# Attention with a mixture of experts on one core: routing rounds seven slots apart in the steady phases, digit sums over 128 rows, and weight subtractions and token low parts at other steps

## The chip, the cores and the metric

The kernel runs on one core of one Trainium2 chip. The metric is the device time of one execution in microseconds (us), the median of the timed runs. Engines: PE is TensorE, DVE is VectorE, ACT is ScalarE, POOL is GpSimd, SP is SyncE.

## The reference

```python
def reference(**inputs):                       # cut
    # attention: 4 batches, 8 heads, 768 positions, head size 64; a query sees the keys
    # whose 6 signs of k @ proj are the same as those of q @ proj
    x = attn_out.transpose(0, 2, 1, 3).reshape(3072, 512)
    logits = x @ w_gate                        # 3072 tokens, 8 experts
    order = np.argsort(-logits.flatten())
    for idx in order:                          # greedy: the best pairs first
        tok, e = idx // 8, idx % 8
        if assigned[tok] >= 0 or counts[e] >= 384: continue
        assigned[tok] = e; counts[e] += 1
    for e in range(8):
        h = np.maximum(x[assigned == e] @ w1[e], 0)    # 512 -> 1024
        out[assigned == e] = h @ w2[e]                 # 1024 -> 512
```

The assignment is greedy over all 24,576 logits, each expert takes 384 tokens, and the products are kept close to fp32 by splitting each operand into an fp16 high part and an fp16 low part.

## The kernel before

**Attention** fills the first 430 us or so. A written table puts its work at numbered steps; constants for the experts' part are made there too, one every four half steps from 89 on (`late`, L350), most of them on POOL.

**Experts.** The greedy assignment is done in eight phases. A phase finds the expert that is full next, its threshold logit, and the 384 tokens that it gets. A threshold is a key of 32 bits, found in six digits (`WID`, 7 bits and then five times 5): a *round* for a digit compares (L493, DVE, `zcmp`), counts per expert by matmul (L504 for the first digit, L511 for others), subtracts from what is left (L513, L514), marks which thresholds are passed (L589) and whether any is (L590, `zhit`), sums the marks over partitions with a one column matmul (the digit sum, L593), and adds the digit to the key (L597, DVE, `zd`). For the digits after the first the marks lie in 32 partitions, and the digit sum reads 32 rows. After the last digit L607 and L608 sum once more, L613 to L631 on DVE work out who is a member (L700 the rows of the expert's weights), L634 and L635 number the members on PE, L643 and L669 build one-hot tables on DVE, L645 collects the token indices on PE, and L661 to L667 close the phase; the next phase starts with L475 to L493.

**Stages and slots.** While phase p is routed, the tokens of the expert before go through its two layers on PE. This is a *stage* of 68 slots: slots 0 to 31 are `layer1` (three matmuls of 384 columns each, L775), slots 32 to 67 `layer2` (two matmuls of 512 columns each, L787). Phase p is spread over stage p-1 and the end of the stage before. `run` puts everything else at slots by tables: `EV[p]=(c0,R)` gives a phase's first slot and the distance R of its rounds, the count of round l at `c0+6+R*l` and its digit sum at `c0+9+R*l`; then come the last sum, L634 and L645 (phase 1 has its own table `E1`; phases 5 and later use `EV[0]`). All engines execute their own instructions in the order of the slots, so an instruction that waits holds up all behind it on its engine.

**Weights.** `wload` fetches an expert's w1 (2 MB) with an indirect DMA from POOL's queue (L716) as soon as the phase knows the expert (L700); ACT splits it in four quarters (L725 the high part, L726 the scaled copy), and the low part is `f - h`, eight subtractions of 128x512 for each weight. These wait in a list, `s.pend`. Three places take from it: `fill` (one subtraction on DVE, L741), `hand` (so many on POOL after a digit's compare, L737, by the tables `H1` and `HS`; the one element copy L736, `ztick`, makes POOL wait for that compare), and the due slot (L847, POOL: whatever is not taken by then). ACT also makes the digits' scaled copies for DVE (L579, `zE`), the tokens' high parts (L750, `xh`), the relu (L777, `hh`) and the outputs (L790); DVE makes the low parts of tokens (L751, `xl`) and of the hidden layer (L778, `hl`).

```python
def hand(s,n):
    n=min(n,len(s.pend))
    if n: s.nc.gpsimd.tensor_copy(s.z([1,1],F32,"tick"),s.gate)
    for _ in range(n): s.nc.gpsimd.tensor_tensor(*s.pend.pop(0)[1],op=ALU.subtract)
```

Of the kernel before, what the change touches and what calls it, by code (L numbers as in the profile page):

```python
# [380 lines left out]
E1=[-12,-4,-3,2,6,8,10,13,16,19,22,25,28,31,34,37,42,49]  # L381
H1=[0,0,0,0,0,1,0,2,0,2,0,2,0,2,0,0,0,0]
EV=[(-17,8),(0,0),(-5,7),(-8,7),(-12,7)]
WL=[4,46]
# [5 lines left out]
XS=[56,56,57,57]  # L390
XD=[0,8,7,4]
KW=[1,0,4,0,2,19,7,1]
SC=16
XSC=8.0
WSC=64.0
class Moe:
# [6 lines left out]
    def consts(s):  # L403
# [33 lines left out]
        todo.append(lambda: G_.tensor_scalar(s.wtb,wt,-32.0,2.0**-44,op0=ALU.add,op1=ALU.mult))  # L437
        s.tiny=fill([128,1],2.0**-32,"tiny",BF).to_broadcast([128,128])

        s.gp=cp.tile([128,2,2,NC],BF,name="gp")  # L440
# [98 lines left out]
    def phase(s,ph):  # L539
# [9 lines left out]
        if not last:  # L549
# [13 lines left out]
            for l,w in enumerate(WID):  # L563
# [3 lines left out]
                if l==0 or first:  # L567
                    for c0,c1_ in blocks if first else ((0,NC),):
                        if l: s.compare(cmp,l,d,c0,c1_)
                        s.count(pc,P,cmp,l,c0,c1_)  # L570
                    if first:
                        if l==0: wp=s.wps(); s.warm(KW[7],wp)
                        s.warm(KW[0],wp)
                    for a,b in ((l+1,l+2),) if first else ((1,6),):
                        if a<6:
                            for q in range(a,b): s.digit(P,q,slice(0,NC))
                            if first: V.tensor_tensor(E[:,a:b],D[:,a:b],s.sc[:,a:b],op=ALU.mult)
                            else:
                                for q in range(a,b): nc.scalar.activation(E[:,q],D[:,q],AF.Copy,scale=2.0**-sum(WID[:q+1]))  # L579
                                s.fill()  # L580
                else:
                    nt=s.count4(pc,P,cmp)

                if l==5: break
                sat=t([128,8],BF,"sat"); hit=t([128,1],BF,"hit"); J=NT[l]
                if l==0 or first:
# [5 lines left out]
                pn=ps(); n=pn[:,0:1]  # L592
                T.matmul(n,s.us[l][0:J],hit[0:J],start=True,stop=True)  # L593
                if first: s.warm(KW[1],wp)
                elif l==0: s.fill()
                d2=t([128,NC],BF,"d2",bufs=6); s.gate=d2[0:1,0:1]
# [4 lines left out]

            sat=t([128,8],BF,"satl"); s.gate=sat[0:1,0:1]; nn=t([128,1],F32,"nn"); nf=t([128,1],F32,"nf")
            if first: V.tensor_scalar(sat[0:32],pc[0:32,0:8],0.0,None,op0=ALU.is_ge)
# [3 lines left out]
            T.matmul(pe[:,0:8],s.ones,s.wtb,start=True,stop=False)  # L607
            T.matmul(pe[:,0:8],s.tiny[0:32],sat[0:32],start=False,stop=True)  # L608
            if first: s.warm(KW[2],wp)
# [133 lines left out]
    def xsplit(s,ph,d):  # L743
        if d==0:
            s.W[ph,'x']=(s.t([128,4,384],F16,"xh",bufs=1),s.t([128,4,384],F16,"xl",bufs=1))
        xh,xl=s.W[ph,'x']
        px=s.psX.tile([128,512],F32,name="px")
        for c in range(3):
            s.nc.tensor.transpose(px[:,c*128:c*128+128],s.XG[ph][:,c,d*128:d*128+128],s.identf)
        s.nc.scalar.mul(xh[:,d],px[:,0:384],XSC)  # L750
        s.lag.append((s.now+3,lambda: s.nc.vector.scalar_tensor_tensor(xl[:,d],px[:,0:384],XSC,xh[:,d],op0=ALU.mult,op1=ALU.subtract)))  # L751

# [63 lines left out]
    def run(s):  # L816
# [7 lines left out]
        for p in range(1,8):  # L824
# [3 lines left out]
            for l in range(4): c+=[c0+6+R*l,c0+9+R*l]  # L828
            c+=[c0+6+4*R,c0+9+4*R,c0+15+4*R,c0+23+4*R]
            ev=[b+e for e in (E1 if p==1 else c)]  # L830
            hs=H1 if p==1 else HS
            dec=ev[-3]
# [72 lines left out]
```

## Time and profile before

| | |
|---|---|
| median of 3 runs | 759.65 us (759.64 to 762.48) |
| the profiled execution's own time | 763.7 us |
| its span, first to last instruction | 761.9 us |
| mean granted TensorE clock | 0.966 of full speed |
| busy share | PE 90%, DVE 72%, POOL 65%, ACT 61%, PEld 58% |
| the expert part with its eight stages | from 444.3 us to 753.5 us |

The shares are means over stretches with different limits. The experts' part is read stage by stage: how long a stage is, what PE waits for in it, and what that engine waits for in turn.

### The profile page before, as it was taken

The numbers are of one execution on the slowest core, as the hardware profiler recorded it, in microseconds if no ns is written. First come the engines' busy times: TensorE is split into PE (matmuls) and PEld (weight loads), VectorE is DVE, ScalarE is ACT, GpSimd is POOL, SyncE is SP. The second block draws the span as 40 slices with busy tenths as digits, with TensorE's granted clock in tenths as the row PEclk, the third lists the DMA queues.
The fourth block names the chain that finished last, engine by engine and source line by source line (L and its number), as shares of the span: only waits on it lengthen the run. The fifth ranks groups of instructions, "written<-read, shape, count | busy, mean of one in ns | idle before, by whom it ended". The sixth has DMA issues, their size and how long they took to land. (4 is left out here: it accounts for less than half of the span.)

```text
span 761.9 us, 19025 instructions
## 1 busy us (share of the span) xinstructions
PE 687.1 (90%) x7789; PEld 440.1 (58%) x7789; DVE 550.4 (72%) x1180; ACT 465.7 (61%) x852; POOL 493.2 (65%) x431
## 2 busy tenths in 40 slices
PE   8898889999999999997888669988989899999995
PEld 2566666767767677675566445544545455555452
DVE  4879968889888898987765666788777878653120
ACT  6677665777776777754554063755646475756550
POOL 8596849696886968855564236374747383858661
PEclk9999999999999999999999569999999999999999
DMA  7638653526445274330001250707071617162711
GB/s 187 174 107 207 154 153 97 149 74 165 133 110 137 74 176 121 88 76 22 22 12 34 65 199 17 261 29 268 37 257 48 220 72 265 43 232 84 260 44 41
DMA packets 39951, 93.57 MB, mean 123 GB/s; under 512 B 4548, under 2 KB 30520, under 8 KB 37816
## 3 DMA queue, kind: packets, MB, share of 16 engines
q1 hardware_dynamic: 33048, 46.21, 23.2%
q0 software_dynamic: 6816, 46.15, 17.3%
q8 instruction: 61, 1.00, 0.6%
q14 instruction: 26, 0.21, 0.1%
HBM read 59.53 MB, written 12.58 MB: 95 GB/s over the span
## 5 line engine op out<-in xcount | busy, mean ns | idle before, releaser
L255 POOL TENSOR_TENSOR lo<-pt 128x768 f16<-128x768 f32 x143 | 233.5, 1646 | 81.5 <-ACT pt L252 72.1
L252 ACT ACTIVATE pt<-pst 128x384 f32<-128x384 f32 x384 | 182.8, 491 | 97.8 <-PE pst L251 85.0
L228 DVE TENSOR_REDUCE m<-pss 128x1 f16<-128x770 f32 x192 | 182.5, 956 | 43.5 <-PE pss L226 42.1
L250 PE MATMUL pst<-qa,ka 128*128 128x384 f16 x384 | 125.9, 328 | 5.5 <-DVE XT L294 3.1
L251 PE MATMUL pst<-qb,kb 128*128 128x384 f16 x384 | 125.9, 328 | 0.0
L267 PE MATMUL psv<-vh,lo 128*128 128x65 f16 x1152 | 122.0, 195 | 3.4 <-POOL lo L255 3.4
L266 PE MATMUL psv<-vl,pt 128*128 128x64 f16 x1152 | 122.2, 194 | 0.0
L265 PE MATMUL psv<-vh,pt 128*128 128x65 f16 x1152 | 122.2, 195 | 0.0
L265 PEld LDWEIGHTS <-pt 128*128 128x128 bf16 x1152 | 107.3, 98 | 12.9 <-issue 3.5
L266 PEld LDWEIGHTS <-pt 128*128 128x128 bf16 x1152 | 106.4, 99 | 9.8 <-issue 0.3
L226 PE MATMUL pss<-ka,qa 128*128 128x385 f16 x384 | 95.3, 330 | 14.9 <-DVE m L228 13.3
L267 PEld LDWEIGHTS <-lo 128*128 128x128 f16 x1152 | 106.5, 98 | 3.7 <-POOL lo L255 3.6
L725 ACT ACTIVATE wh<-wf 128x1024 f16<-128x1024 f32 x64 | 67.2, 1050 | 39.8 <-PE psa L693 21.1
L737 POOL TENSOR_TENSOR wl<-wf,wh 128x512 f16<-128x512 f32 x64 | 72.1, 1146 | 0.0
L775 PEld LDWEIGHTS <-wh 128*128 128x128 f16 x512 | 48.3, 98 | 37.2 <-issue 8.3
L726 ACT ACTIVATE wf<-wf 128x1024 f32<-128x1024 f32 x62 | 65.5, 1057 | 2.0
L778 DVE SCALAR_TENSOR_TENSOR hl<-px,hh 128x384 f16<-128x384 f32 x64 | 34.7, 552 | 42.7 <-ACT hh L777 42.3
L226 PEld LDWEIGHTS <-qa 128*128 128x128 f16 x384 | 37.5, 98 | 46.6 <-issue 24.3
L787 PEld LDWEIGHTS <-hh 128*128 128x128 f16 x384 | 36.7, 99 | 43.5 <-issue 6.3
L255 DVE TENSOR_TENSOR lo<-pt 128x768 f16<-128x768 f32 x49 | 60.8, 1241 | 1.5 <-ACT pt L252 1.0
L790 ACT ACTIVATE o<-po 128x512 f32<-128x512 f32 x24 | 14.3, 594 | 70.4 <-PE po L787 70.3
L775 PE MATMUL px<-xh,wh 128*128 128x384 f16 x256 | 55.5, 329 | 1.7 <-DVE xl L751 1.4
(250 smaller groups left out, 1334.5 us busy)
## 6 DMA issues: line engine op xcount, KB each, us to landing
vp<-in_vv_dram SPq DMA_DIRECT2D x8, 768.0 KB
x_dram<-X SPq DMA_DIRECT2D x16, 384.0 KB
qp<-in_qT_dram SPq DMA_DIRECT2D x7, 768.0 KB
kp<-in_kT_dram SPq DMA_DIRECT2D x7, 768.0 KB
qa<-qh SPq DMA_DIRECT2D x14, 192.0 KB
ka<-kh SPq DMA_DIRECT2D x14, 192.0 KB
qb<-qh SPq DMA_DIRECT2D x14, 192.0 KB
kb<-kh SPq DMA_DIRECT2D x14, 192.0 KB
```

Of the source, the lines that this page charges most:

```text
L226: T.matmul(ps[:,hf,0:HK],QA[u][:,j,qc*128:qc*128+128],KA[u][:,j,hf*HK:hf*HK+HK],start=True,stop=True)
L228: V.tensor_reduce(M6[h][:,qc:qc+1],ps[:,:,0:HK],axis=AX.XY,op=ALU.max,negate=True)
L250: T.matmul(ps[:,0:384],KA[u][:,j,kr],QA[u][:,j,r],start=True,stop=False)
L251: T.matmul(ps[:,0:384],KB[u][:,j,kr],QB[u][:,j,r],start=False,stop=True)
L252: A.activation(PT[h,kc][0][:,r],ps[:,0:384],AF.Exp,scale=0.125)
L255: eng.tensor_tensor(l,p,p.bitcast(BF)[:,1::2],op=ALU.subtract)
L265: T.matmul(av[:,c,:],ph[:,r],VH[u][:,j,kc,:],start=(kc==0 and c==0),stop=False,skip_group_check=True)
L266: T.matmul(av[:,c,0:64],ph[:,r],VL[u][:,j,kc,:],start=False,stop=False,skip_group_check=True)
L267: T.matmul(av[:,c,:],l[:,r],VH[u][:,j,kc,:],start=False,stop=False,skip_group_check=True)
L725: s.nc.scalar.mul(h[:,r],f[:,r],WSC)
L737: for _ in range(n): s.nc.gpsimd.tensor_tensor(*s.pend.pop(0)[1],op=ALU.subtract)
L775: T.matmul(p[:,0:384],a[:,o:o+128],b[:,d],start=n==0,stop=n==11)
```

## The change

- Phases 5 and 6 (`EV[0]`): rounds 7 slots apart, not 8. The last sum is then at slot 20 of the stage (24 before), L634 at 26 (30), L645 at 35 (38), for phase 7 too. In phases 2 to 4 L645 comes one slot later.
- Digit sums after the first digit, and the last sum, read 128 rows: `hit` and `satl` are kept tiles whose other rows are zero, made by three more memsets on POOL among the constants.
- Weight subtractions: phase 1 hands 2, 2, 2, 3, 3 to POOL (1, 2, 2, 2, 2 before) and takes none on DVE in its first digit; phases 2 and 3 hand 3, 3, 3, 4 (2, 3, 3, 3 before). Phases 4 and later keep `HS`.
- Tokens: phase 1's transposes come two slots later; the low parts `xl` follow the transposes after one slot (phase 1) or two, not three.

```diff
-H1=[0,0,0,0,0,1,0,2,0,2,0,2,0,2,0,0,0,0]
-EV=[(-17,8),(0,0),(-5,7),(-8,7),(-12,7)]
+H1=[0,0,0,0,0,2,0,2,0,2,0,3,0,3,0,0,0,0]
+H2=[0,0,0,3,0,3,0,3,0,4,0,0,0,0]
+EV=[(-17,7),(0,0),(-5,7),(-8,7),(-12,7)]
-XD=[0,8,7,4]
+XD=[0,10,7,4]
+        s.hits=[fill([128,1],0.0,f"hit{i}",BF) for i in range(2)]; s.satl=fill([128,8],0.0,"satl",BF)
-                                s.fill()
+                                if ph>1: s.fill()
-                sat=t([128,8],BF,"sat"); hit=t([128,1],BF,"hit"); J=NT[l]
+                sat=t([128,8],BF,"sat"); hit=t([128,1],BF,"hit") if l==0 or first else s.hits[l%2]; J=NT[l]
-                T.matmul(n,s.us[l][0:J],hit[0:J],start=True,stop=True)
+                T.matmul(n,s.us[l][0:J if first else 128],hit[0:J if first else 128],start=True,stop=True)
-                elif l==0: s.fill()
+                elif l==0 and ph>1: s.fill()
-            sat=t([128,8],BF,"satl"); s.gate=sat[0:1,0:1]; nn=t([128,1],F32,"nn"); nf=t([128,1],F32,"nf")
+            sat=s.satl; s.gate=sat[0:1,0:1]; nn=t([128,1],F32,"nn"); nf=t([128,1],F32,"nf")
-            T.matmul(pe[:,0:8],s.tiny[0:32],sat[0:32],start=False,stop=True)
+            T.matmul(pe[:,0:8],s.tiny,sat,start=False,stop=True)
-        s.lag.append((s.now+3,lambda: s.nc.vector.scalar_tensor_tensor(xl[:,d],px[:,0:384],XSC,xh[:,d],op0=ALU.mult,op1=ALU.subtract)))
+        s.lag.append((s.now+(1 if ph==1 else 2),lambda: s.nc.vector.scalar_tensor_tensor(xl[:,d],px[:,0:384],XSC,xh[:,d],op0=ALU.mult,op1=ALU.subtract)))
-            c+=[c0+6+4*R,c0+9+4*R,c0+15+4*R,c0+23+4*R]
+            c+=[c0+6+4*R,c0+9+4*R,c0+15+4*R,c0+24+4*R]
-            hs=H1 if p==1 else HS
+            hs=H1 if p==1 else H2 if p<4 else HS
```

On POOL, phase 2 in stage 1, before: the ticks are L736, the subtractions L737 and, by the due slot, L847; L796 sends an output, and L716 is the load of the next w1.

```order
L736 CAST ztick<-zcmp_380 1x1
L737 TENSOR_TENSOR wl_9273<-wf_9147,wh_9272 128x512 x2
L796 DMA out_dram<-o,zidx 3072x512
L736 CAST ztick<-zcmp_381 1x1
L737 TENSOR_TENSOR wl_9273<-wf_9147,wh_9272 128x512 x3
L796 DMA out_dram<-o,zidx 3072x512
L736 CAST ztick<-zcmp_380 1x1
L737 TENSOR_TENSOR wl_9273<-wf_9147,wh_9272 128x512
L737 TENSOR_TENSOR wl_9404<-wf_9251,wh_9403 128x512 x2
L736 CAST ztick<-zcmp_381 1x1
L737 TENSOR_TENSOR wl_9404<-wf_9251,wh_9403 128x512 x3
L716 DMA wf_9645<-in_w_dram,zwidx 128x4096
L847 TENSOR_TENSOR wl_9404<-wf_9251,wh_9403 128x512 x2
```

The same place after the change (the changed file's lines stand two further down: L738 and L739 are the tick and the subtraction, L798 the output, L718 the load):

```order
L738 CAST ztick<-zcmp_383 1x1
L739 TENSOR_TENSOR wl_9273<-wf_9148,wh_9272 128x512 x3
L798 DMA out_dram<-o,zidx 3072x512
L738 CAST ztick<-zcmp_384 1x1
L739 TENSOR_TENSOR wl_9273<-wf_9148,wh_9272 128x512 x3
L798 DMA out_dram<-o,zidx 3072x512
L738 CAST ztick<-zcmp_383 1x1
L739 TENSOR_TENSOR wl_9403<-wf_9251,wh_9402 128x512 x3
L738 CAST ztick<-zcmp_384 1x1
L739 TENSOR_TENSOR wl_9403<-wf_9251,wh_9402 128x512 x4
L718 DMA wf_9642<-in_w_dram,zwidx 128x4096
```

The two subtractions behind the load are gone; one moved into the first batch and one into the last, which stands ahead of the load.

On DVE, the second and third digit of phase 5, at slots 57 to 60 of stage 3, before:

```order
L513 TENSOR_TENSOR znt<-rem,psa 32x8
L514 TENSOR_TENSOR znt<-znt,psa 32x8 x2
L589 TENSOR_TENSOR zsat<-psa,znt 32x8
L590 TENSOR_REDUCE zhit<-zsat 32x1
L751 SCALAR_TENSOR_TENSOR xl<-px,xh 128x384 x2
L597 SCALAR_TENSOR_TENSOR zd_10909<-zd_10848,psa,zE 128x24
L493 TENSOR_TENSOR zcmp_380<-zd_10909,tb_94 128x768
L751 SCALAR_TENSOR_TENSOR xl<-px,xh 128x384 x2
```

And after (L599 is the key's new digit, L495 the compare, L753 the low part of tokens):

```order
L515 TENSOR_TENSOR znt<-rem,psa 32x8
L516 TENSOR_TENSOR znt<-znt,psa 32x8 x2
L591 TENSOR_TENSOR zsat<-psa,znt 32x8
L592 TENSOR_REDUCE hit_90<-zsat 32x1
L753 SCALAR_TENSOR_TENSOR xl<-px,xh 128x384 x4
L599 SCALAR_TENSOR_TENSOR zd_10895<-zd_10833,psa,zE 128x24
L495 TENSOR_TENSOR zcmp_383<-zd_10895,tb_97 128x768
```

All four token low parts now stand ahead of the key's next digit and its compare, two did before.

## Rows read from the trace of the kernel before

**Rows 1.** The windows view of stages 0 to 6 (start and end in us, length, busy time and instructions of each engine, granted clock, share and rate of the DMAs).

```profile
444.26:489.63 45.37, 39.02 (x296) 21.27 (x295) 31.79 (x116) 24.69 (x40) 18.69 (x21) 0.92 0.43 150
489.63:532.69 43.06, 37.38 (x275) 19.90 (x275) 33.10 (x101) 25.50 (x40) 24.05 (x25) 1.00 0.42 147
532.69:573.95 41.26, 38.14 (x270) 20.43 (x270) 31.45 (x98) 24.29 (x38) 23.73 (x25) 0.96 0.43 149
573.95:614.26 40.31, 37.19 (x277) 19.92 (x276) 32.98 (x105) 23.70 (x36) 22.78 (x25) 1.00 0.40 138
614.26:651.02 36.76, 35.97 (x271) 19.96 (x270) 28.23 (x97) 23.60 (x37) 21.48 (x24) 1.00 0.45 158
651.02:685.64 34.62, 34.62 (x230) 19.08 (x230) 20.97 (x71) 22.62 (x31) 24.78 (x27) 1.00 0.42 144
685.64:722.08 36.44, 34.99 (x207) 18.90 (x206) 10.64 (x20) 22.60 (x32) 25.92 (x25) 0.95 0.43 160
```

**Rows 2.** The timeline of POOL: the ticks of phases 1 and 2, the last batch of phase 2, and the loads of w1 for phases 1 to 3 (start us, duration us, what; in brackets the idle time before it and what ended it).

```profile
466.38 0.17 POOL L736 CAST ztick<-zcmp 1x1 f32<-1x1 bf16 x1 [0.88 <-DVE zcmp L493]
469.66 0.17 POOL L736 CAST ztick<-zcmp 1x1 f32<-1x1 bf16 x1 [0.89 <-DVE zcmp L493]
...
473.20 0.97 POOL L716 DMA_INDIRECT wf<-in_w_dram,zwidx  x1 [1.14 <-DVE zcum L631]
...
504.25 0.18 POOL L736 CAST ztick<-zcmp 1x1 f32<-1x1 bf16 x1
...
508.54 0.17 POOL L736 CAST ztick<-zcmp 1x1 f32<-1x1 bf16 x1 [0.77 <-DVE zcmp L493]
508.67 3.37 POOL L737 TENSOR_TENSOR wl<-wf,wh 128x512 f16<-128x512 f32 x3
513.41 1.33 POOL L716 DMA_INDIRECT wf<-in_w_dram,zwidx  x1 [1.37 <-DVE hl L778]
...
552.61 0.99 POOL L716 DMA_INDIRECT wf<-in_w_dram,zwidx  x1 [1.58 <-DVE hl L778]
```

**Rows 3.** The timeline of ACT in the same stages: the first split of each w1, the output it waits for at the end of stage 2, and the last token part of stage 2.

```profile
482.32 1.05 ACT L725 ACTIVATE wh<-wf 128x1024 f16<-128x1024 f32 x1
...
522.71 1.06 ACT L725 ACTIVATE wh<-wf 128x1024 f16<-128x1024 f32 x1 [4.62 <-DVE zeq L478]
...
533.04 0.47 ACT L750 ACTIVATE xh<-px 128x384 f16<-128x384 f32 x1
...
561.40 1.06 ACT L725 ACTIVATE wh<-wf 128x1024 f16<-128x1024 f32 x1 [1.02 <-DVE zkey L477]
...
566.65 0.60 ACT L790 ACTIVATE o<-po 128x512 f32<-128x512 f32 x1 [1.07 <-PE po L787]
```

**Rows 4.** The timeline of DVE: three instructions with two inputs in SBUF that start while POOL runs a batch of subtractions.

```profile
505.91 1.90 DVE L597 SCALAR_TENSOR_TENSOR zd<-zd,psa,zE 128x24 bf16<-128x24 bf16 x1 [0.66 <-PE psa L593]
...
584.76 1.70 DVE L597 SCALAR_TENSOR_TENSOR zd<-zd,psa,zE 128x24 bf16<-128x24 bf16 x1
...
510.74 0.23 DVE L613 SCALAR_TENSOR_TENSOR zwg<-zd,znn,zmxu 128x24 f32<-128x24 bf16 x1
```

**Rows 5.** The timeline of POOL: the batches that the first two of these meet.

```profile
504.40 3.36 POOL L737 TENSOR_TENSOR wl<-wf,wh 128x512 f16<-128x512 f32 x3
...
583.03 3.38 POOL L737 TENSOR_TENSOR wl<-wf,wh 128x512 f16<-128x512 f32 x3
```

**Rows 6.** The timeline of PE around two digit sums, of 32 rows and of 128 (the part of the array in use stands ahead of the shape).

```profile
580.29 0.33 PE L775 MATMUL px<-xl,wh 128*128 128x384 f16 x1
580.54 0.17 PE L593 MATMUL psa<-zhit,us 32*128 32x1 bf16 x1
580.65 0.66 PE L775 MATMUL px<-xl,wh 128*128 128x384 f16 x3
...
606.17 0.17 PE L593 MATMUL psa<-zhit,us 128*128 128x1 bf16 x1
606.20 1.02 PE L787 MATMUL po<-wl,hh 128*128 128x512 f16 x4
```

**Rows 7.** The timeline of PE in stages 2 to 6: first and last digit step of phases 4 and 5, the waits that stand behind, and stage 6's wait with the matmuls after it.

```profile
572.54 0.17 PE L593 MATMUL psa<-zhit,us 32*128 32x1 bf16 x1
...
592.38 0.20 PE L634 MATMUL psa<-zSTb,ntri 128*128 128x48 bf16 x1 [0.27 <-DVE zwidx L700]
...
610.34 0.17 PE L593 MATMUL psa<-zhit,us 32*128 32x1 bf16 x1
...
629.99 0.19 PE L634 MATMUL psa<-zSTb,ntri 128*128 128x48 bf16 x1
...
640.99 0.76 PE L504 MATMUL psa<-zOH,zcmp 128*128 128x8 bf16 x24 [0.79 <-DVE zcmp L493]
...
705.50 0.79 PE L645 MATMUL psa<-zRr,ohp 128*128 128x12 bf16 x24 [1.45 <-DVE zRr L669]
...
707.00 3.52 PE L787 MATMUL po<-wl,hh 128*128 128x512 f16 x8
```

**Rows 8.** The costliest groups of PE's instructions from 444 us on, those that wait most or are the digit sums (count, busy us, mean ns, idle us before and what ended it).

```profile
L787 PE MATMUL po<-wl,hh 128*128 128x512 f16 x192 | 48.5, 389 | 2.1 <-POOL wl L847 2.1
...
L645 PE MATMUL psa<-zRr,ohp 128*128 128x12 bf16 x168 | 5.6, 183 | 6.0 <-DVE zRr L669 6.0
```

**Rows 9.** The windows view of a stretch in stage 2 in which the granted clock is half (columns as in the first group).

```profile
560.40:563.70 3.30, 3.30 (x9) 1.18 (x8) 3.27 (x13) 2.27 (x3) 2.46 (x3) 0.50 0.51 132
```

## The prediction

> **What bounds the kernel now.** I read the windows by stage first, then the timelines of PE, POOL, DVE and ACT. The reader is to see that the stages are not alike [rows 1]. Stage 5 takes 34.6 us and PE is busy throughout, so that is what a stage costs without waits. Stages 0 to 3 take 45.4, 43.1, 41.3 and 40.3 us, and PE idles there, mostly for DVE: 6.0 us for the one-hot tables of L669 alone, and 2.1 us for low parts that POOL makes at the due slot [rows 8].
>
> Behind these waits two things run in a loop. First, a round can't go faster than POOL's batch. The key's next digit (L597, two inputs in SBUF) that starts inside a batch of three subtractions ends when the whole batch has ended: it starts at 505.91 and takes 1.90 us to 507.81, the batch runs from 504.40 to 507.76; the same at 584.76 (to 586.46) and the batch to 586.41 [rows 4, 5]. Without a batch in its way the same kind takes a quarter of a microsecond. So one turn (tick, batch, digit, compare, next tick) lasts 508.54-504.25 = 4.29 us with three subtractions, and 469.66-466.38 = 3.28 us with two, where PE's slots set the pace anyhow [rows 2]. One subtraction is 3.37/3 = 1.12 us.
>
> The Trainium skill, "SBUF — State Buffer", section "SBUF: two separate sides", calls the port pair that both engines share an exclusive lock, held for the whole instruction, that a DVE operation with two SBUF inputs needs too. That agrees with the block, but by it the lock is free between two subtractions; both rows passed such a gap and were not let in.
>
> Second, the end of the rounds starts the load of the next w1. The loads are issued at 473.20, 513.41 and 552.61, and ACT's first split starts at 482.32, 522.71 and 561.40 [rows 2, 3]: 8.8 to 9.3 us later each time, with ACT idle before the last two. Three or four splits on, ACT makes the next phase's digits and token parts. A load issued later makes all of that later.
>
> **The change part by part.** The sum is made on the profiled execution (span 761.9, own time 763.7 us); the median is 759.65, so I add the difference to the median.
>
> *More subtractions in phases 1 to 3.* Phase 1: no subtractions on DVE in the first digit. They took about 0.6 us of the chain there, of which I count 0.5 as gained since PE's slots pace the next rounds. Its last two batches have three instead of two: the turn between them becomes 4.3 instead of 3.3 (+1.0), and the last sum's work (L613) stands behind one more subtraction (+1.1). The load comes 1.0+1.1-0.5 = 1.6 us later. ACT is then late at the start of stage 1, where PE already waits for it; I take 1.5. Phase 2: the first batch's third subtraction is hidden, since ACT's late relu holds the next digit up longer; the last batch's fourth is not: +1.1. At the start of stage 2 the last token part on ACT (533.04) stands behind that load's splits [rows 3], and the digit behind its low part, so all of it arrives. Phase 3: first and last batch both count, +2.2, but ACT waits 1.07 us for PE's output between its splits [rows 3], and that slack is used up first: +1.1. Together 1.5+1.1+1.1 = +3.7 us at phase 4's rounds. Below: nothing, if ACT and PE have that much slack; above: 2.1+1.1+2.2 plus 0.6 for the tails = 6.
>
> What this removes is the due-slot subtractions, and with them PE's waits for low parts (2.1 us in all) and part of the waits for L669 (a block of DVE ahead of the tables). I cost that gain at nothing in stages 0 to 2: PE then waits for the first digit or token part instead, which hang on the load. Where the load is not what is late, the gain is real; that is the first rival.
>
> *Rounds seven slots apart, and the token low parts.* Phase 4 is the model: R=7, the same table of batches, all four low parts ahead of its second digit sum's digit. From that digit sum to L634, 34 slots, it takes 592.38-572.54 = 19.84 us. Phase 5 takes 629.99-610.34 = 19.65 us for the same path, but over 38 slots [rows 7]. So seven slots don't make the path shorter, POOL's batches set it, and four layer-1 slots are left to be done after it: 12 matmuls at 0.162 us (0.65 for four starts, less the tail) = 1.95 us. With the 0.19 that is +2.1 us a phase. Given back: in stage 4 the next phase's first count (L504) no longer waits, since it now stands 16 slots behind L645, not 13 (0.8 idle on PE plus its late weight load, 0.95 in all, and 0.15 at L645): 2.1-1.1 = +1.0. In stage 5 no count follows: +2.1-0.1 = +2.0. Bounds for both together: 1.4 (a path of 19.4, since phase 4's was held up by an output) and 4.2 (nothing given back).
>
> *Stage 6.* Only phase 7's end is there. PE waits 1.45 us for L669 at 705.50, and right after it eight matmuls take 3.52 us [rows 7], at a granted clock of one half, the 1.2 GHz level, as in stage 2 [rows 9]; at full clock they take 1.89 there, so 1.63 us more. L645 now stands 9 slots behind L634 and mostly among longer layer-1 slots: 6*0.487+3*0.432 = 4.2 us against 2*0.487+6*0.432 = 3.6, and DVE's step meets POOL's batch four slots earlier. I take wait and low clock as gone, 1.45+1.63+0.1 = -3.2 us. Bounds: 0 and -3.3.
>
> *Digit sums.* With 32 rows PE starts the sum 0.25 us after a matmul that takes 0.16 and goes on 0.11 later; with 128 it goes on 0.03 later [rows 6]: 0.17 us saved each. There are 24 such sums and 6 last sums, 4.9 us at most. But within rounds POOL's batch sets the pace, and PE would only wait longer. I count two or three that lie outside: -0.4. Bounds 0 and -4.9.
>
> The Trainium skill, "TensorE: Matmul & The Clock Gate", section "Why this matters for your kernels", says that a single matmul over 32 rows takes as long as one over 128. Its "TensorEngine Tiling (Array Packing)", "Key Properties", says that a change of tiling mode drains the engine. The rows side with the second. By the first the digit sums would give nothing and the sum would be 0.4 us higher.
>
> *Constants.* Three small memsets on POOL and twelve half steps' delay of others lie beside attention's work: +0.2, bounds 0 and 0.5.
>
> Sum: 3.7+1.0+2.0-3.2-0.4+0.2 = +3.3 us. Median 759.65+3.3 = **763.0 us**. All bounds at once give 0+1.4-3.3-4.9 = -6.8 and 6+4.2+0.5 = +10.7, that is 752.9 to 770.4.
>
> **The rivals.**
>
> *DVE gets in between two subtractions.* L613 at 510.74 took 0.23 us inside the batch that runs from 508.67 [rows 2, 4]. If that is the rule in the new order, a batch costs the digit one subtraction at most: the load is not later (the 3.7 go, and about 1.5 of waits in stages 0 to 2 are gained), the rounds follow PE (stages 4 and 5 lose 3.0 of loss and gain the 1.1 given back and 0.17*10 of sums). 3.3-3.7-1.5-3.0-1.1-1.7 = -7.7, that is 752 us. The skill's page on SBUF says the same, lock by instruction. Against it stand two rows of long blocks across a gap. 15%.
>
> *Slower: the new stalls halve the clock.* At the starts of stages 1, 2 and 3 PE waits for ACT and DVE in one piece, by the sum above nearly 3 us each. In stage 2 a wait of that kind was followed by the half clock [rows 9], at 1.6 us. Where PE has slack behind the stall nothing follows; where the count of the next digit arrives later than its compare, each costs its 1.6. Three give +4.9, that is 768 us. 18%.
>
> *Little changes: the load's delay meets slack.* If ACT's queue absorbs phases 1 and 2, 1.5+1.1 fall away and 760.4 us is left. 17%.
>
> **How the numbers follow.** The forecast has 50%, with its own range 760 to 766. About 0.5%, 3.8 us, is what a measurement of this kernel can tell from no change; slower then begins at 763.45, so the forecast is split: 0.26 same, 0.24 slower. The first rival gives 0.13 faster and 0.02 same; the second 0.18 slower; the third 0.14 same and 0.03 faster. Sums: faster 0.16, same 0.42, slower 0.42. The range for 8 in 10 leaves out the lower half of the first rival and the upper part of the second: 754.5 to 768.
>
> **What would show it.** In the trace after: loads of w1 issued 1.6, 2.7 and about 5 us later for phases 1 to 3, the first splits 9 us behind them, PE idle before the first matmuls of stage 1 and before counts at the end of stages 1 and 2; L597 ending with POOL's batches; waits of PE for the compare in stages 4 and 5, none at L504; stage 6 near 33.2 us with a granted clock of 1. Wrong: loads not later, or rounds in stages 4 and 5 in 3.6 us, or stage 6 still with its wait.

## Result and the profile after

The changed kernel takes 766.77 us, median of 7 runs (765.47 to 768.96), against 759.65 us (757.42 to 762.48). The ratio is 1.0096, with a 95% interval of 1.0073 to 1.0119: it is slower by 5.5 to 9 us. The forecast was 763.0 us, with a range of 754.5 to 768.0.

The profiled execution took 767.9 us, with a span of 766.1 us. The windows of its eight stages, columns as in [rows 1]:

```profile
444.70:489.03 44.33, 37.04 (x295) 20.47 (x295) 31.88 (x114) 25.01 (x42) 20.68 (x23) 1.00 0.43 157
489.03:531.30 42.27, 36.50 (x275) 19.73 (x275) 31.02 (x98) 23.70 (x38) 24.03 (x25) 1.00 0.39 141
531.30:574.61 43.31, 36.37 (x272) 19.71 (x271) 33.99 (x100) 25.07 (x39) 24.18 (x25) 1.00 0.38 135
574.61:617.13 42.52, 37.79 (x278) 20.21 (x277) 34.55 (x107) 23.79 (x37) 22.64 (x25) 0.96 0.37 131
617.13:655.11 37.98, 35.24 (x271) 19.70 (x270) 31.55 (x98) 23.60 (x36) 21.80 (x24) 1.00 0.43 153
655.11:691.25 36.14, 34.06 (x231) 18.87 (x230) 24.03 (x71) 22.97 (x31) 25.67 (x27) 1.00 0.43 149
691.25:726.28 35.03, 33.29 (x207) 18.46 (x206) 11.06 (x20) 22.46 (x32) 25.70 (x25) 1.00 0.42 154
726.28:757.58 31.30, 31.30 (x169) 16.32 (x167) 4.18 (x8) 13.25 (x20) 16.90 (x16) 1.00 0.17 70
```

Against [rows 1], stages 2 to 5 are longer, stages 0, 1 and 6 shorter. But the granted clock differs too: 0.92, 0.96 and 0.95 in stages 0, 2 and 6 before, 1.00 in all three now, and the other way round in stage 3, 0.96 now. So part of what looks like a gain belongs to the one execution that was profiled; a second profile of the kernel before, below, separates that.

What PE waits for, from the timeline of PE (in brackets the idle time before the instruction and what ended it; lines stand two further down than before):

```profile
489.03 0.65 PE L777 MATMUL px<-xh,wh 128*128 128x384 f16 x3 [2.60 <-DVE xl L753]
...
530.28 0.32 PE L513 MATMUL psa<-zOH,zcmp 128*128 128x32 bf16 x6 [2.60 <-DVE zcmp L495]
...
554.25 0.20 PE L636 MATMUL psa<-zSTb,ntri 128*128 128x48 bf16 x1 [1.61 <-DVE zwidx L702]
...
599.29 0.39 PE L789 MATMUL po<-wh,hl 128*128 128x512 f16 x1 [1.53 <-DVE hl L780]
...
661.50 0.32 PE L513 MATMUL psa<-zOH,zcmp 128*128 128x32 bf16 x6 [1.18 <-DVE zcmp L495]
...
666.16 0.32 PE L513 MATMUL psa<-zOH,zcmp 128*128 128x32 bf16 x6 [0.90 <-DVE zcmp L495]
...
710.09 0.79 PE L647 MATMUL psa<-zRr,ohp 128*128 128x12 bf16 x24 [1.74 <-DVE zRr L671]
```

The waits of [rows 8] for the low parts of the due slot are gone, and so are those for the one-hot tables in stages 1 and 2. In their place PE waits 2.6 us for the token part at the start of stage 1, 2.6 us for the compare at its end, and 1.6 us for the numbering in stage 2. In stage 5 (and the same in stage 4) it waits for the compare at slots 10 and 17. The wait for the table in stage 6 is still there, 1.74 us.

POOL's timeline, the loads of w1 for phases 1 to 3 and the rounds of phase 6:

```profile
472.20 0.97 POOL L718 DMA_INDIRECT wf<-in_w_dram,zwidx  x1 [0.82 <-DVE zcum L633]
...
513.09 1.33 POOL L718 DMA_INDIRECT wf<-in_w_dram,zwidx  x1 [1.21 <-DVE hl L780]
...
555.07 0.99 POOL L718 DMA_INDIRECT wf<-in_w_dram,zwidx  x1 [1.58 <-DVE hl L780]
...
657.16 0.18 POOL L738 CAST ztick<-zcmp 1x1 f32<-1x1 bf16 x1
657.30 3.38 POOL L739 TENSOR_TENSOR wl<-wf,wh 128x512 f16<-128x512 f32 x3
661.88 0.18 POOL L738 CAST ztick<-zcmp 1x1 f32<-1x1 bf16 x1
...
666.17 0.17 POOL L738 CAST ztick<-zcmp 1x1 f32<-1x1 bf16 x1 [0.77 <-DVE zcmp L495]
```

The turn between ticks is 4.72 and 4.29 us, though the slots stand one closer. With rounds eight slots apart it was the same, 4.71 and 4.29, as POOL's ticks of phase 6 in the kernel before show:

```profile
652.29 0.18 POOL L736 CAST ztick<-zcmp 1x1 f32<-1x1 bf16 x1
...
657.00 0.18 POOL L736 CAST ztick<-zcmp 1x1 f32<-1x1 bf16 x1
...
661.29 0.17 POOL L736 CAST ztick<-zcmp 1x1 f32<-1x1 bf16 x1 [0.77 <-DVE zcmp L493]
```

And, in the changed kernel, the key's next digit on DVE, beside a batch of phase 1 and one of phase 6:

```profile
465.92 0.39 DVE L599 SCALAR_TENSOR_TENSOR zd<-zd,psa,zE 128x24 bf16<-128x24 bf16 x1
...
658.82 1.91 DVE L599 SCALAR_TENSOR_TENSOR zd<-zd,psa,zE 128x24 bf16<-128x24 bf16 x1
```

The second starts inside the batch of 657.30 and ends at 660.73, as the batch does (660.68). The first is an exception that comes up again at the end.

### The profile page after: what moved, and what is told of

It reads as the page before. It is cut to its first block, busy times and chain, and to the rows that moved or that the text cites. A ratio compares the mean times of both kernels' runs of the same rounds, so it can differ in the third digit from the quotient of the medians.

```text
span 766.1 us, 19028 instructions
## 1 busy us (share of the span) xinstructions
PE 676.6 (88%) x7789; PEld 435.9 (57%) x7789; DVE 561.6 (73%) x1178; ACT 464.9 (61%) x852; POOL 496.7 (65%) x436
## 5 line engine op out<-in xcount | busy, mean ns | idle before, releaser
L228 DVE TENSOR_REDUCE m<-pss 128x1 f16<-128x770 f32 x192 | 182.5, 956 | 40.1 <-PE pss L226 39.1
L739 POOL TENSOR_TENSOR wl<-wf,wh 128x512 f16<-128x512 f32 x71 | 79.9, 1146 | 0.0
L777 PE MATMUL px<-xh,wh 128*128 128x384 f16 x256 | 53.5, 326 | 5.3 <-DVE xl L753 2.6
## 6 DMA issues: line engine op xcount, KB each, us to landing
vp<-in_vv_dram SPq DMA_DIRECT2D x8, 768.0 KB
qp<-in_qT_dram SPq DMA_DIRECT2D x7, 768.0 KB
kp<-in_kT_dram SPq DMA_DIRECT2D x7, 768.0 KB
```

The lines of the kernel that those rows point to most:

```text
L228: V.tensor_reduce(M6[h][:,qc:qc+1],ps[:,:,0:HK],axis=AX.XY,op=ALU.max,negate=True)
L777: T.matmul(p[:,0:384],a[:,o:o+128],b[:,d],start=n==0,stop=n==11)
```

## The experiments

The theory after the result: batches of subtractions on POOL, by which DVE's operations with two SBUF inputs are held up, set the turn of a round; longer batches and closer slots therefore give waits, not speed. Against it stood the rivals of the prediction, and three open points: the parts add up to more than the forecast, stage 6, and the attention part, which I had not suspected.

### The parts alone

Each of the four parts was put into the kernel before by itself.

The digit sums (diff shortened):

```diff
+        s.hits=[fill([128,1],0.0,f"hit{i}",BF) for i in range(2)]; s.satl=fill([128,8],0.0,"satl",BF)
-                T.matmul(n,s.us[l][0:J],hit[0:J],start=True,stop=True)
+                T.matmul(n,s.us[l][0:J if first else 128],hit[0:J if first else 128],start=True,stop=True)
```

> The kernel before with one part of the change: the digit sums after the first digit, and the last sum, read 128 rows of kept tiles. My account (batches of subtractions set the pace of the rounds, so most of the shorter sums only lengthens PE's wait): -0.4 us for the sums, +0.2 us for three more constants, 759.5 us, and the sums' own matmuls no longer start 0.25 us late. Rival (the drain before and after each sum is on the path everywhere): 30 times 0.17 = 5 us less, 754.8 us. Rival (128 rows cost what 32 do): 759.7 us.

Measured: 761.47 us, ratio 1.0022 (1.0007 to 1.0038). None of the three. A gain within the experts' part, if any, is smaller than a loss elsewhere. Most of the loss sits in attention: from row maximum 152 to 160 (L228, counted from 0) it takes 16.56 us in this kernel and 16.57 in the changed one, instead of 15.33. The timelines of DVE and PE in the changed kernel at that place, and then that of POOL (`lo` is a low part in attention, `m` the row maximum):

```profile
302.89 2.23 DVE L255 TENSOR_TENSOR lo<-pt 128x768 f16<-128x768 f32 x1
...
306.05 0.51 PE L138 MATMUL pss<-qp,pr 128*32 128x384 f32 x1 [0.83 <-DVE m L228]
```

```profile
300.71 1.47 POOL L255 TENSOR_TENSOR lo<-pt 128x768 f16<-128x768 f32 x1
302.11 0.10 POOL L414 MEMSET nrem<- 128x8 f16 x1
302.84 5.03 POOL L255 TENSOR_TENSOR lo<-pt 128x768 f16<-128x768 f32 x3 [0.63 <-ACT pt L252]
```

The last constant, twelve half steps later than before, now lies between POOL's low parts, and the one ahead of it one low part earlier. DVE's own low part starts 0.05 us after POOL's next batch and takes 2.23 us, and PE waits for the row maximum behind it.

The rounds:

```diff
-EV=[(-17,8),(0,0),(-5,7),(-8,7),(-12,7)]
+EV=[(-17,7),(0,0),(-5,7),(-8,7),(-12,7)]
-            c+=[c0+6+4*R,c0+9+4*R,c0+15+4*R,c0+23+4*R]
+            c+=[c0+6+4*R,c0+9+4*R,c0+15+4*R,c0+24+4*R]
```

> The kernel before with one part: rounds seven slots apart in phases 5 and 6, and the tables' L634 and L645 that go with it. My account: +1.0 us in stage 4, +2.0 us in stage 5, -3.2 us in stage 6, so 759.5 us, with waits of PE at the counts of phases 5 and 6 and none for the one-hot tables in stage 6. Rival (stage 6 keeps its wait and the half clock behind it): 762.6 us. Rival (DVE gets in between subtractions, so rounds follow PE): 756 us.

Measured: 762.96 us, ratio 1.0031 (1.0017 to 1.0045): the rival. Stage 4 takes 37.2 us and stage 5 35.9, and stage 6 keeps its wait:

```profile
703.83 0.79 PE L645 MATMUL psa<-zRr,ohp 128*128 128x12 bf16 x24 [1.78 <-DVE zRr L669]
```

The subtractions:

```diff
-H1=[0,0,0,0,0,1,0,2,0,2,0,2,0,2,0,0,0,0]
+H1=[0,0,0,0,0,2,0,2,0,2,0,3,0,3,0,0,0,0]
+H2=[0,0,0,3,0,3,0,3,0,4,0,0,0,0]
-            hs=H1 if p==1 else HS
+            hs=H1 if p==1 else H2 if p<4 else HS
```

> The kernel before with one part: more of phases 1 to 3's weight subtractions handed to POOL within the rounds, none on DVE in phase 1's first digit. My account: the loads of the next w1 come 1.6, 1.1 and 2.2 us later, the time rises by 3.7 us to 763.4 us. The measured change (+7.1 us for all parts) would put more here, 765 us, if waits of stages 2 and 3 come from this part. Rival (the delay meets slack on ACT): 760.8 us. Rival (DVE gets in between subtractions): 758 us.

Measured: 763.07 us, ratio 1.0040 (1.0028 to 1.0053), +3.0 us: my account, within its bounds.

The tokens (diff shortened):

```diff
-XD=[0,8,7,4]
+XD=[0,10,7,4]
-        s.lag.append((s.now+3, ...
+        s.lag.append((s.now+(1 if ph==1 else 2), ...
```

> The kernel before with one part: phase 1's transposes two slots later, and token low parts on DVE one or two slots behind the transposes, not three. My account gives this part nothing by itself in stages 0 to 3 and up to 0.3 us where a low part stands ahead of the key's next digit: 759.7 us, at most 760.5. Rival (the low parts delay the digit and PE stalls, or PE gets its first token parts earlier): 762 us, or 757 us.

Measured: 761.80 us, ratio 1.0015 (0.9999 to 1.0031); +1.1 us, with an interval that ends at nothing, so between my account and the first rival. In its profile stages 4 and 5 take 37.5 and 35.3 us, 0.7 and 0.6 more than before. About half of that is in small waits of PE (0.06 to 0.17 us each at slots 65, 21 and 38) that the kernel before has not; the rest is not traced.

The four ratios add up to 1.0108, the whole is 1.0096. The intervals of the five together leave some 0.004 open, so no interplay of the parts is to be seen, and a small one is not excluded.

### A second profile of the kernel before

> The kernel before, unchanged, for a second profile. If the half clock stretches in the first profile (three in the expert part, one at 348 us) are a matter of the single execution, this one has other stretches, a time near 760 us, and stage lengths that agree within 0.3 us wherever neither execution has a stretch in the stage. Rival (the stretches belong to the kernel): stretches at 451, 560 and 707 us again, 763.7 us.

The kernel is unchanged. It took 759.85 us. Its windows, stage by stage:

```profile
442.13:486.77 44.64, 38.78 (x296) 21.18 (x295) 31.79 (x116) 24.69 (x40) 18.95 (x22) 0.96 0.44 154
486.77:529.87 43.10, 37.39 (x276) 19.92 (x276) 33.15 (x101) 25.48 (x40) 24.11 (x25) 1.00 0.43 148
529.87:571.64 41.77, 38.19 (x270) 20.47 (x270) 31.47 (x98) 24.33 (x38) 23.78 (x25) 0.96 0.43 147
571.64:611.87 40.23, 37.19 (x277) 19.93 (x276) 32.98 (x105) 23.71 (x36) 22.81 (x25) 1.00 0.40 138
611.87:648.64 36.77, 35.98 (x271) 19.97 (x270) 28.39 (x97) 23.60 (x37) 21.52 (x24) 1.00 0.45 158
648.64:683.27 34.63, 34.63 (x230) 19.08 (x230) 21.12 (x71) 22.94 (x31) 24.93 (x27) 1.00 0.44 150
683.27:717.40 34.13, 33.29 (x207) 18.50 (x206) 10.49 (x20) 21.01 (x31) 24.25 (x24) 1.00 0.40 144
717.40:749.50 32.10, 31.63 (x169) 16.33 (x167) 4.18 (x8) 14.71 (x21) 18.43 (x17) 1.00 0.21 89
```

Stages 1, 3, 4 and 5 agree within 0.1 us with [rows 1]. Stage 6 does not: 34.13 us at full clock instead of 36.44 at 0.95, while stage 7 takes 32.10 instead of 31.30. The rival holds for most of the half clock: it is there again at about 348 us and in stages 0 and 2 (0.96 in both windows). The expectation holds for the time, and for stage 6. So the half clock in stage 6 that I had counted as a cost of the kernel was one of that execution; stages 6 and 7 together take 66.2 us here, and 66.3 in the changed kernel. The one in stage 2 is not of that kind: it is there in both profiles of before.

### The constants

The changed kernel, with the three zero tiles made in the step that makes `tiny` (diff shortened):

```diff
-        s.hits=[fill([128,1],0.0,f"hit{i}",BF) for i in range(2)]; s.satl=fill([128,8],0.0,"satl",BF)
+        def zeros():
+            f0()
+            for z in s.hits+[s.satl]: G_.memset(z,0.0)
+        todo.append(zeros)
```

> The changed kernel, but the three zero tiles are made in the step that makes tiny, so that no later constant is delayed. If the 1.24 us that attention loses between its 152nd and 160th row maximum come from the later constants (memsets among POOL's subtractions), the loss goes and the time falls from 766.8 to 765.5 us, ratio 1.0080. Rival (the loss is not from the constants' steps): ratio 1.0096 as before, the loss still there.

Measured: 766.07 us, ratio 1.0071 (1.0047 to 1.0094). The 1.24 us in attention are gone (15.32 us between the two row maxima, 15.33 before), and the same low part of DVE is no longer held up; it starts at the same 302.63 us as POOL's batch, not after it:

```profile
302.63 0.94 DVE L255 TENSOR_TENSOR lo<-pt 128x768 f16<-128x768 f32 x1
```

The ratio falls by 0.0025, which is what 1.24 us and a little more would do, but the intervals overlap: the trace shows the cause, the times agree with it and don't prove it. The Trainium skill, "SBUF — State Buffer", section "SBUF: two separate sides", says that whichever of the two engines starts first gets the pair; the start that came 0.05 us later and was held fits that. What happens at equal starts the section does not say, and a row of phase 7, below, does not fit, if the start of its record is the one that counts.

### Shorter batches, the work left for later

The changed kernel, where phases 5 to 7 hand over 2, 2, 2, 2 instead of 2, 3, 3, 3:

```diff
+H5=[0,0,0,2,0,2,0,2,0,2,0,0,0,0]
-            hs=H1 if p==1 else H2 if p<4 else HS
+            hs=H1 if p==1 else H2 if p<4 else HS if p<5 else H5
```

> The changed kernel, but phases 5 to 7 hand over 2, 2, 2, 2 subtractions instead of 2, 3, 3, 3, the other three at the due slot. If a batch of three sets the pace of the rounds, a turn falls from 4.3 to below 3.6 us, PE's waits for the compare at slots 10 and 17 of stages 4 and 5 (1.16 and 0.90 us each time) go, and the two stages take 1.5 to 2 us less each: 763 us. Rival (the wait is for PE's and DVE's own chain): waits and time as in the changed kernel, 766.8 us. Third (the late subtractions make layer 2 wait): the waits at the counts go, PE waits for wl instead, 766 us or more.

Measured: 777.36 us, ratio 1.0232 (1.0209 to 1.0256). POOL's ticks in stage 5, and from the timeline of PE what it waits for there:

```profile
661.62 0.18 POOL L739 CAST ztick<-zcmp 1x1 f32<-1x1 bf16 x1
...
665.23 0.18 POOL L739 CAST ztick<-zcmp 1x1 f32<-1x1 bf16 x1
...
668.41 0.17 POOL L739 CAST ztick<-zcmp 1x1 f32<-1x1 bf16 x1 [0.77 <-DVE zcmp L496]
```

```profile
684.78 0.58 PE L790 MATMUL po<-wl,hh 128*128 128x512 f16 x1 [3.21 <-POOL wl L850]
```

The turn fell from 4.72 and 4.29 to 3.61 and 3.18 us, and the waits at slots 10 and 17 from 1.18 and 0.90 to 0.04 us and nothing: the batch does set the pace. But layer 2 needs the low parts two slots behind the due slot, PE waits 3 to 4 us for them, and the half clock follows (0.92 for stage 5). The third expectation held in kind, and was far too mild.

### Phase 7 at three places

Nothing but the place of the numbering and the collection of phase 7 in the kernel before; first at slots 12 and 24 of stage 6:

```diff
-            if p==7: ev=ev[-2:]; hs=[0,0]
+            if p==7: ev=[b+12,b+24]; hs=[0,0]
```

> The kernel before, but phase 7's numbering (L634) stands at slot 12 of stage 6 and its collection (L645) at slot 24, not at 30 and 38. If the wait of 0.8 to 1.5 us at L645 comes from DVE meeting a token's low part and a batch of subtractions between the two slots, twelve slots cover it: wait gone, stage 6 near 33.1 us at full clock, time 758.5 us where a half clock had followed in part of the executions (1.7 us more). Rival (stages 6 and 7 share another limit, as stage 7's waits at slots 16 and 20 where stage 6 was short): stage 7 gets longer by what stage 6 loses, 760 us.

Measured: 766.91 us, ratio 1.0093 (1.0069 to 1.0117). The wait at L645 grew to 5.98 us. DVE's `zmi` starts 0.02 us ahead of a batch of four and is held to the batch's end all the same. DVE's row, and POOL's:

```profile
690.51 4.55 DVE L649 TENSOR_SCALAR zmi<-zpm 128x24 int32<-128x24 int32 x1
```

```profile
690.53 4.49 POOL L847 TENSOR_TENSOR wl<-wf,wh 128x512 f16<-128x512 f32 x4
```

Then at slots 46 and 54 of stage 5, where I had seen no subtractions:

```diff
+            if p==7: ev=[b-22,b-14]; hs=[0,0]
```

> The kernel before, but phase 7's numbering and collection at slots 46 and 54 of stage 5, where POOL runs no subtractions. If the wait at L645 in stage 6 is DVE blocked by batches (1.6 to 1.9 us at 30 and 38, 4.6 and 2.0 us at 12 and 24), it is gone here, no half clock can follow it, and the time falls by 0.8 us, by 1.5 more in executions that had the half clock: 758.5 us. Rival (stage 7 takes what stage 6 gives): 760 us.

Measured: 761.16 us, ratio 1.0029 (1.0012 to 1.0045). I had overlooked that from phase 6 on the splits' subtractions are issued at once, in this place too. DVE's row, and POOL's:

```profile
675.17 2.44 DVE L669 TENSOR_TENSOR zRr<-zGt,gp 128x144 bf16<-128x144 f32 x2
```

```profile
674.35 3.08 POOL L847 TENSOR_TENSOR wl<-wf,wh 128x512 f16<-128x512 f32 x2 [0.61 <-issue]
```

Both expectations failed, by the mechanism that they were meant to avoid. With the places of the two kernels (30 and 38, 26 and 35) that makes four in which the wait is DVE held by a batch: 0.84 us in the second profile above, 1.74 in the changed kernel, 5.98 and 1.45 here.

### The due-slot subtractions on DVE

The change removes the due-slot subtractions of phases 1 to 3 by longer batches. Here they go without that: DVE does them behind `zcum`.

```diff
         V.tensor_tensor_scan(cum,s.one48,STb,0.0,op0=ALU.mult,op1=ALU.add); s.gate=cum[0:1,0:1]
+        for _ in range((0,1,2,2)[ph] if ph<4 else 0): s.fill()
```

> The kernel before, but the one or two subtractions that phases 1 to 3 leave for the due slot are done on DVE right behind the scan (zcum) that closes the members' marks: no batch of POOL is longer, the loads of w1 keep their place. This takes apart what the change did to these phases in one step: the due-slot subtractions go, the batches do not grow. If the due-slot subtractions cause PE's waits for wl (0.78, 0.65 and 0.73 us) and part of those for the one-hot tables (1.2 and 2.8 us), and if what the change lost is the longer batches, then these waits go and the time falls by 2 to 4 us, to 757 us. Rival (stages 1 to 3 hang on the loads alone): the gain comes back as a wait at the next stage's start, 760 us. Third (1.4 us more on DVE delays the numbering): 761.5 us.

Measured: 757.98 us, ratio 0.9988 (0.9973 to 1.0002): between the first and the second expectation. PE's waits for `wl` at L787 are gone; that for the table falls from 1.2 to 0.4 us in stage 1 and from 2.8 to 1.7 in stage 2, and 1.3 us come back as a wait for the compare at the end of stage 1 and 0.7 as one for `hl` within it. DVE does two of them in little more than POOL does one:

```profile
509.80 1.27 DVE L742 TENSOR_TENSOR wl<-wf,wh 128x512 f16<-128x512 f32 x2
```

The edit just shown, phase 7 at slots 46 and 54 of stage 5, and the digit sums with their zero tiles made in the step of `tiny`, together (diff shortened):

```diff
+        for _ in range((0,1,2,2)[ph] if ph<4 else 0): s.fill()
+            if p==7: ev=[b-22,b-14]; hs=[0,0]
+                T.matmul(n,s.us[l][0:J if first else 128],hit[0:J if first else 128],start=True,stop=True)
```

> The kernel before with the two edits of the other runs of this call and the digit sums over 128 rows, their zero tiles made in the step that makes tiny. If the sums by themselves gain 0.4 to 0.7 us in the expert part and their loss was the later constants alone, this is 0.5 us better than the two edits added: 755 us if each does what is expected of it, 759.5 us if only the sums do.

Measured: 759.80 us, ratio 1.0013 (0.9998 to 1.0027). The two edits alone add to 1.0017, so what is left for the digit sums is -0.0004, with an uncertainty of some 0.0025 (three intervals of 0.0015 each): 0.3 us less, plus or minus 2. If the three edits simply add, a gain of 4.9 us, which their rows would have allowed, is excluded; that of 0.4 is neither shown nor refuted.

### Shorter batches, the work on DVE

The kernel of the due-slot subtractions, with one of three subtractions of a batch taken by DVE in phases 2 to 4 (diff shortened; `step` hands the phase on):

```diff
     def hand(s,n,ph=0):
         n=min(n,len(s.pend))
         if n: s.nc.gpsimd.tensor_copy(s.z([1,1],F32,"tick"),s.gate)
+        if n>2 and 1<ph<5: s.fill(); n-=1
```

> The kernel of e9_fills, and in phases 2 to 4 one subtraction of each batch of three is done on DVE right behind the compare (0.68 us there), so POOL runs two. If POOL's batch sets the turn of a round, the turn falls from 4.3 to about 3.7 us (0.68 + 2 times 1.12 + 0.75 of chain), the loads of w1 in stages 1 to 3 come 1.5 to 2 us earlier within their stage, PE's waits for the compare in these stages (0.6 to 0.8 us each) shrink, and the time falls by 2 to 4 us against e9_fills, to 755 us. Rival (DVE is the longer chain once it does the subtraction): turn 4.2 us or more, 758 us or above. Third (rounds get shorter, but stages hang on ACT and the weights' landing): turn 3.7 us, time 757.5 us.

Measured: 751.13 us, ratio 0.9883 (0.9859 to 0.9907). The ticks of phase 2 with a batch in POOL's timeline, and the windows of stages 1 to 3:

```profile
496.89 0.57 POOL L737 CAST ztick<-zcmp 1x1 f32<-1x1 bf16 x1 [2.42 <-DVE zcmp L493]
497.44 2.26 POOL L739 TENSOR_TENSOR wl<-wf,wh 128x512 f16<-128x512 f32 x2
500.87 0.23 POOL L737 CAST ztick<-zcmp 1x1 f32<-1x1 bf16 x1
...
504.09 0.58 POOL L737 CAST ztick<-zcmp 1x1 f32<-1x1 bf16 x1 [0.77 <-DVE zcmp L493]
```

```profile
486.33:527.28 40.95, 36.97 (x275) 19.95 (x275) 29.94 (x106) 25.87 (x40) 19.73 (x20) 1.00 0.45 163
527.28:565.82 38.54, 36.24 (x270) 20.05 (x270) 29.45 (x102) 24.29 (x38) 19.87 (x20) 1.00 0.42 152
565.82:603.97 38.15, 36.34 (x278) 20.03 (x276) 31.01 (x109) 23.74 (x38) 20.22 (x22) 1.00 0.42 146
```

The two turns from tick to tick take 3.98 and 3.22 us, where the kernel without this edit, that of the due-slot subtractions, has 4.70 and 4.29. Its stages 1 to 3 take 43.6, 40.0 and 40.2 us, so here they are 2.6, 1.5 and 2.0 us shorter, all of them at full clock. The load of w1 goes out at 22.2 and 18.4 us of stages 1 and 2, not at 24.4 and 20.2. The gain is larger than the forecast because it returns in every turn of the loop: load to load, 37.8, 37.1 and 37.0 us now, against 40.0, 39.4 and 39.0. This version beats both kernels.

## Why the prediction was right and wrong

The time lay in the range and on the side to which the sum pointed, but the sum was 4 us short: +3.3 where 7.1 was measured. Two steps failed, and they are most of the difference: stage 6, where 3.2 us were to be gained, and the constants in attention. One of the prediction's three signs of being wrong came true, "stage 6 still with its wait"; the other two, loads not later and rounds of 3.6 us in stages 4 and 5, did not. The lengths below are from the profiles of all kernels in which the stages' code is that of before (for stages 0 to 3 both profiles of before and the two with phase 7 moved; for stages 6 and 7 both profiles of before and the kernels with the sums, the subtractions, the tokens and the due-slot subtractions alone) or that of after (the changed kernel, that with the constants moved, and for stages 0 to 3 that with light batches).

| term | forecast | measured | by |
|---|---|---|---|
| loads later, stages 0 to 3 | +3.7 | +3.9 | 169.0 us on average (167.7 to 170.0, 4 profiles) to 172.8 (172.4 to 173.6, 3 profiles); the part alone +3.0 in the time |
| rounds, stage 4 | +1.0 | +1.2 | 36.8 to 38.0 |
| rounds, stage 5 | +2.0 | +1.5 | 34.6 to 36.1 |
| phase 7, stages 6 and 7 | -3.2 | -0.5 | 66.8 (66.2 to 67.7, 6 profiles) to 66.3 (2 profiles); nothing at the same clock, see below |
| constants, attention | +0.2 | +1.24 | 15.33 to 16.57 between two row maxima |
| digit sums | -0.4 | within the others | not resolved by the runs |
| sum | +3.3 | +7.3 | medians: +7.1 |

**More subtractions in phases 1 to 3.** The sum of 3.7 was right, and the part alone gives +3.0 in the time. The step "the rounds can't go faster than POOL's batch" holds: with the batch unchanged closer slots left the turn as it was (4.71 and 4.29 us at eight slots, 4.72 and 4.29 at seven) and gave only waits, and taking a third of the batch away cut the turn, once at a price elsewhere and once for a gain of some 7 to 8 us over the same kernel without it. "The end of the rounds starts the load" holds as well: from load to first split it is 8.7 to 9.6 us for phases 1 to 3 in every profile.

How much later phase 1's load is issued is seen only at the same granted clock, since stage 0 has none, one or two stretches of 3.4 us at half clock, and the load moves with them. Counted from the start of stage 0, with one stretch it goes out after 26.9, 27.2 and 28.2 us (phase 7 moved, and the second profile of before), and after 28.5 and 29.6 in the kernels with the longer batches (light batches, constants moved). With two stretches in a row it is 28.9 (first profile of before) against 30.5 (the subtractions alone). Both ways that is 1.6 us, as forecast, though from few profiles; the profile of the changed kernel, 27.5, had no stretch. From the first load to the third it takes 82.9 and 83.0 us against 79.4 and 80.0, 3.2 more, where the prediction had 1.1 and 2.2. Of that, 1.2 us are given back by the fourth load. The prediction had 1.07, by ACT's slack, but that is not shown: in the four profiles with the code of before a stretch at half clock lies between the third load and the fourth, in the three with longer batches none does, and such a stretch had cost 1.6 us in stage 6.

The slot by which L645 comes later in phases 2 to 4 was named in the prediction and not priced. In stage 3 PE then waits for `hl` behind the one-hot tables (599.29 above, 1.53 us; 1.53 also with the rounds' part alone). It costs nothing by itself: with that part alone this wait stands in place of 0.63 us for the table and most of 0.98 for the next phase's first count, and stage 3 takes 40.2 us, as in the profiles of before (40.3 and 40.2).

**What the due-slot subtractions give back.** I had put their gain at nothing, since PE would wait for the token part and the first digit instead. That is what the rows show: 2.60 us for `xl`, 2.60 for the compare, 1.12 for `xh`, where waits for low parts and tables had been.

**The rounds of stages 4 and 5.** Right in kind and size: 2.7 us for 3.0. No wait is left at the next phase's first count in stage 4, as forecast, and the new waits stand at slots 64, 10 and 17. The tokens' low parts have their share: by themselves they make the two stages 0.7 and 0.6 us longer, the rounds by themselves 0.5 and 1.2, which I had not separated.

**Stage 6.** Here the step failed that says "I take wait and low clock as gone". The wait is not gone: L634 and the step behind it still meet a batch of POOL, since one lies between slots 26 and 35 as well, and it holds DVE for 2.3 us. DVE's row in the changed kernel, and POOL's:

```profile
705.22 2.33 DVE L651 TENSOR_SCALAR zmi<-zpm 128x24 int32<-128x24 int32 x1
```

```profile
705.24 2.27 POOL L849 TENSOR_TENSOR wl<-wf,wh 128x512 f16<-128x512 f32 x2
```

Four slots earlier is not four slots clear of the batches; I had counted the time between the two slots, and had not laid POOL's row beside it. The half clock behind it, 1.6 us of the 3.2, was a matter of the execution: the same stage ran at full clock in the second profile of before and in the parts with the subtractions or the tokens alone, and at half clock for a while with the sums alone. The new places don't rule it out either: with the rounds alone stage 6 has it again (0.95), and stages 6 and 7 take 68.1 us. Set against each other at the same clock, the old places take 66.4 us on average without the half clock and 67.7 with it, the new ones 66.3 and 68.1. So the step gave nothing that these profiles show, and the -0.5 of the table is the mix of clocks in its profiles.

**The base.** That is also a fault of the frame of the sum. The profiled execution was 4 us above the median, and I took from it a gain that a typical execution has not to give. A term that rests on a low clock has to be weighed by how often it appears, or left out of a sum that is added to the median.

**Constants.** +0.2 with bounds 0 and 0.5, measured 1.24. I had added up durations of small memsets; what counts is whom they let go first. The rule that I used all through the experts' part, that a DVE operation waits for POOL's instruction, holds in attention too (2.23 us for a low part that takes 0.94 when not held), and I had not asked there.

**Digit sums.** The bound of 4.9 us, which the rows of single sums allow, is refuted. The rows agree with the reason given, that POOL's batch takes what PE saves: with the sums alone the turns of stage 4 are still 4.7 and 4.3 us, and PE waits 0.24 us for a compare within the rounds there, where it waited for none.

**The rivals.** "DVE gets in between two subtractions" did not decide the time. It happens, more often than the one row that I had: in the trace after, a DVE operation stood waiting at 22 boundaries between two subtractions of a batch, and was let in at 7 of them. "The new stalls halve the clock" came about in part. With the longer batches, three of four profiles (the subtractions alone, the constants moved, light batches) have a stretch at half clock just after the start of stage 1 and one across its end, behind a wait of PE for the compare of 2.4 to 2.6 us; the changed kernel's own profile has neither. In exchange the stretch in stage 2, which every profile with the code of before has, is gone. The mean granted clock over the runs hardly moves, 0.972 in the changed kernel and 0.970 to 0.972 in the series of before, so this is not where the 7.1 us come from. "The load's delay meets slack" is not borne out: the loads come later by what was forecast, and the part alone costs 3.0 us.

## What to carry to other kernels

Where two engines hold each other up for whole batches, look at every place where their rows lie side by side, the small ones and those in other parts of the kernel as well, and count a batch as one block; moving an instruction by some slots helps only if POOL's row is empty where it lands. Work that fills an idle engine is not free if a loop waits for the end of the batch: give a piece of it to the engine that would otherwise be held up. And take two profiles before a low clock in one of them becomes a term of a sum.

## What was not expected of the hardware

- **Who is let in between two instructions is not settled by the rows.** DVE's L599 of 465.92 was let in at a boundary inside a batch of three (0.39 us), that of 658.82 passed a boundary and waited to the end (1.91 us). In the trace after, the wait before the boundary is 0.24 to 1.02 us in the 7 cases that were let in and 0.03 to 2.2 us in the 15 that were not. Nor does an early start settle it: `zmi` in the run with phase 7 at slots 12 and 24 began 0.02 us ahead of its batch and was held. What decides it stays open; no run here tries it.
- **An operation with one SBUF input can be held as well**: `zmi` (128x24, int32 to int32) took 4.55 us beside a batch of four, 0.18 without one.
- **The same subtraction (128x512) takes 0.68 us on DVE and 1.12 on POOL.**
- **Stretches at the half clock move from execution to execution** of one kernel: stage 6 of the kernel before has one in its first profile and none in the second. Not all do: the one in stage 2 is in both.
